# RWKV attention and a squared-ReLU layer on one core: steps 3 to 5 transposed by DMA, and new orders from step 3 on

## The chip, the core and the metric

The kernel runs on one core of a Trainium2 chip. The metric is the device time of one execution in microseconds (us). Several runs are taken and their median is the time; one further execution is recorded by the hardware profiler, and its span (first to last instruction) is a little shorter than its own time. The engines are TensorE (PE; PEld is its weight load), VectorE (DVE), ScalarE (ACT), GpSimd (POOL) and SyncE (SP), which here only issues DMAs.

## What is computed

Linear attention with a decaying state, then a layer with a squared ReLU. Batch 4, 8 heads, 768 tokens, 48 numbers a head; the layer goes from 384 to 2048 and back.

```python
def _attn_ref(r, k, v, w, u):
    state = zeros((B, H, D, D))
    for t in range(S):
        cur = einsum('bhd,bhe->bhde', u[None] * kt, vt)
        y[:, :, t] = einsum('bhd,bhde->bhe', rt, state + cur)
        state = wt[:, :, :, None] * state + einsum('bhd,bhe->bhde', kt, vt)

def _moe_ref(x, w_in, w_out):          # x: y as (4 * 768) x (8 * 48)
    h = x @ w_in
    r = maximum(h, 0.0)
    return (r * r) @ w_out
```

## The kernel before

**Steps.** The 3072 tokens go through in twelve steps s = 0 to 11 of 256 tokens, three to a batch. On the 128 partitions lie pairs of neighbouring tokens (j = 0, 1); the partitions are two chunks c of 64. Attention of later steps runs beside the layer of earlier ones.

**An order written out by hand.** The string ORDER (line 17) holds some 900 words, each one operation: a name, step and part, and then `:bank` (the PSUM bank) or `=A`, `=V`, `=G` (ScalarE, VectorE, GpSimd). The loop at line 634 records them in this order under a manual schedule. Each engine runs its own words strictly in the order of the string, and waits where an operand or a buffer isn't ready. SyncE's list too: a DMA whose source isn't ready holds up all DMAs behind it. Buffers are handed out in rotation by `buf` (line 173) in the order of the words: r, k, v and w have four each, rkT two, y_sb two, xT four.

**Attention of a step.** ld loads w, r, k, v (line 201). ww_ (288) multiplies the decays of a pair, lw_ (292) takes the logarithm, cum_ (332 to 336) sums it over the chunk on TensorE, from step 8 on with ni_ (344) on VectorE for one half; exp_ and ac_ (349, 356) take the exponential. rw_ and kw_ (300, 304) apply the decay inside a pair; rd_.s.0 and rd_.s.1 (370) make the decayed r and k. These must be transposed: in steps 0 to 3 by tr_ on TensorE through PSUM (379) and a copy rkt_ (384), from step 4 on by dtr_ (387), a DMA transpose from SBUF to SBUF. p_ (404) makes the scores, pm_ (412, 415) masks them, y_ multiplies by v (v_ at line 296 is its cast), yc_ adds the carried state, and yq_ the token's own term, for which ku_, qp_, q_ and vq_ (307, 312, 315, 318) prepare vq (all three of y at line 450). su_, ts_ and sn_ (426, 436, 440) carry the state on. ysb_ (486, 488) copies y out of PSUM. Then y is transposed: in steps 0 to 5 by yt_ on TensorE (496) and a copy xt_ (500), from step 6 on by dyt_ (503), a DMA transpose.

**The layer of a step.** m1_.s.g (513) makes two of 16 column blocks of h in one PSUM bank; rl_ (520, 522) takes the ReLU, sq_ (528, 530) the square of four blocks. In steps 0 to 4, m2_ (536) multiplies by w_out, os_ (542, 544) scales and store (614) writes out. From step 5 on a form with seven block products takes the place of m2_: sw_ (568) makes sums of blocks of the activations, pw_ (590) the seven products, cx_ and ow_ (595, 597, 609) put them together. tw_.1 to tw_.4 (555) make the sums of the blocks of w_out, once. The weights are loaded and cast at the beginning (221).

**Small-tile products.** p_, su_, y_, yq_ and yc_ use parts of the 128x128 array; m1_, m2_, pw_, tr_, yt_ and cum_ the whole.

Of the kernel before, what the change touches and what calls it, by code (L numbers as in the profile page):

```python
# [39 lines left out]
dtr_.5.0 m1_.3.1:3 qp_.5 ts_.4.1=V m2_.2.1.3 rl_.3.1=A rl_.3.7=V dtr_.5.1 p_.4.1:0 p_.4.0:1 os_.2.1=V m1_.3.3:1  # L40
pm_.4.0 vq_.4 store.1.1 m2_.2.0.2 ld.6.r rl_.3.3=A pm_.4.1 m1_.3.2:2 ld.6.k sn_.4.1 m1_.3.0:3 ld.7.r rl_.3.2=A ww_.6=G
ld.7.k sq_.3.1=A su_.5:1 y_.4:0 ts_.5.0=V ww_.7=G yc_.4 q_.5 yq_.4 store.1.0 p_.5.0:1 ysb_.4=A m1_.3.5:2 ld.6.v
rl_.3.0=V lw_.7 m2_.2.0.3 pm_.5.0 yt_.4:1 os_.2.0=A m1_.3.4:3 ld.8.w xt_.4=V lw_.6 ku_.6 rl_.3.5=V p_.5.1:1 rl_.3.4=A
cum_.7:0 pm_.5.1 ld.8.r m1_.3.6:0 exp_.7 vq_.5 m1_.4.3:1 sq_.3.0=A rw_.7=V ld.7.v cum_.6:1 m1_.4.1:3 rl_.4.3=A kw_.7=G
m1_.4.0:2 rl_.4.1=A store.2.1 m1_.4.5:1 rl_.3.6=A rl_.4.0=V sn_.5.0 exp_.6 m2_.3.1.0:3 rd_.7.0 kw_.6=G sq_.3.2=A
m2_.3.0.0:0 rd_.7.1 m2_.3.0.1 rw_.6=G rl_.4.5=A m2_.3.1.1 sq_.3.3=A ww_.8=G rd_.6.0 m2_.3.0.2 ac_.7 m1_.4.4:1 qp_.6
rd_.6.1 dtr_.6.0 m2_.3.0.3 ac_.6 m1_.4.2:2 v_.6=A dtr_.6.1 ku_.7 q_.6 v_.7=A su_.6:1 y_.5:0 ld.11.w os_.3.0=V yc_.5
ld.9.w rl_.4.4=V vq_.6 yq_.5 ld.8.k m2_.3.1.2 rl_.4.2=V ysb_.5=A m2_.3.1.3 rw_.8=V ts_.6.0=A store.3.0 yt_.5:1 sn_.6.0
ld.8.v os_.3.1=A m1_.4.7:0 xt_.5=A qp_.7 m1_.4.6:3 ts_.6.1=V sq_.4.2=A m1_.5.7:2 rl_.4.6=A p_.6.1:1 rl_.5.7=V
store.0.1 p_.6.0:0 rl_.4.7=A sn_.6.1 m1_.5.0:1 pm_.6.1 lw_.8 m1_.5.1:3 sq_.4.0=A ld.9.k ww_.9=G pm_.6.0 m1_.5.5:0  # L50
rl_.5.1=A m1_.5.4:2 dtr_.7.0 sq_.4.3=A rl_.5.0=V y_.6:1 sq_.4.1=V rl_.5.5=A su_.7:0 yc_.6 rl_.5.4=A kw_.8=V yq_.6 q_.7
m2_.4.0.0:3 ysb_.6=A m1_.5.6:2 v_.8=A ts_.7.0=V dyt_.6 vq_.7 cum_.8:1 rl_.5.6=A m2_.4.1.0:0 ni_.8=V sq_.5.0=A dtr_.7.1
m2_.4.0.1 tw_.1=V sn_.7.0 m2_.4.0.2 ac_.8 exp_.8 store.3.1 m2_.4.0.3 ww_.11=V ld.9.r lw_.9 m1_.5.3:1 ku_.8 os_.4.0=A
ld.10.w rd_.8.1 m2_.4.1.1 sq_.5.2=A ld.9.v m2_.4.1.2 ts_.7.1=V rl_.5.3=A tw_.3=V m1_.5.2:3 dtr_.8.1 qp_.8 m1_.6.3:2
rl_.5.2=A m1_.6.4:1 sq_.5.1=A rd_.8.0 m2_.4.1.3 rl_.6.3=A rl_.6.4=V p_.7.0:1 os_.4.1=A sw_.5.0.1=V p_.7.1:0 ku_.9
sq_.5.3=A dtr_.8.0 m1_.6.0:3 pm_.7.1 m1_.6.2:1 rl_.6.0=A m1_.6.7:0 pm_.7.0 sn_.7.1 m1_.6.1:2 rl_.6.7=A sw_.5.1.1=V
pw_.5.1:3 rl_.6.1=A sw_.5.1.2=V tw_.2=V rl_.6.2=A y_.7:1 su_.8:0 sq_.6.1=A yq_.7 yc_.7 sw_.5.0.2=V pw_.5.2:1 cx_.5.1=A
sw_.5.0.3=V ysb_.7=A sw_.5.1.3=V m1_.6.6:2 sw_.5.1.4=V sq_.6.0=A dyt_.7 sw_.5.0.4=V m1_.6.5:0 ow_.5.1=V tw_.4=V
rl_.6.6=A pw_.5.6 sw_.6.0.1=G store.4.1 rl_.6.5=A cum_.9:1 ld.10.k cx_.5.2=A pw_.5.5 ni_.9=V ld.11.k pw_.5.7 ts_.8.0=V
exp_.9 store.2.0 q_.8 rw_.9=G m1_.7.2:2 cx_.5.3=A ld.10.v ac_.9 m1_.7.5:0 kw_.9=V rl_.7.2=A vq_.8 rd_.9.0 pw_.5.3  # L60
rl_.7.5=A m1_.7.6:2 sq_.6.3=A rd_.9.1 dtr_.9.0 sn_.8.0 m1_.7.1:0 ow_.5.4=V ow_.5.2=V qp_.9 p_.8.0:1 dtr_.9.1 rl_.7.1=A
p_.8.1:0 m1_.7.0:1 sq_.6.2=A pm_.8.1 m1_.7.7:0 rl_.7.6=A ku_.10 pm_.8.0 pw_.5.4 v_.9=A pw_.6.1:2 rl_.7.7=A q_.9
ow_.5.3=A su_.9:1 rl_.7.0=A y_.8:0 sw_.6.1.1=V cx_.6.1=A yc_.8 sw_.6.0.2=V lw_.11 sw_.6.1.2=V yq_.8 ww_.10=V pw_.6.2:1
ysb_.8=A kw_.10=V m1_.7.3:0 ts_.9.0=A sw_.6.1.4=V dyt_.8 sq_.7.3=A ow_.6.1=V m1_.7.4:3 sn_.9.0 rl_.7.3=V pw_.6.6
sw_.6.0.3=G store.5.0 rl_.7.4=A ts_.9.1=V sq_.7.2=A ld.10.r p_.9.1:0 cx_.6.2=V p_.9.0:1 sw_.6.1.3=V ld.11.r vq_.9
pw_.6.5 pm_.9.0 lw_.10 store.4.0 m1_.8.4:0 sq_.7.1=A store.5.1 m1_.8.2:3 sw_.6.0.4=V ld.11.v rl_.8.4=A kw_.11=V
cum_.10:1 cx_.6.3=A pw_.6.7 rw_.10=G rl_.8.2=A ni_.10=V m1_.8.5:0 pm_.9.1 exp_.10 qp_.10 m1_.8.0:3 ac_.10 rd_.10.0
pw_.6.3 rl_.8.0=A cum_.11:0 sq_.7.0=A ow_.6.2=V rw_.11=G m1_.8.3:3 dtr_.10.0 rd_.10.1 m1_.8.1:1 rl_.8.5=A sn_.9.1
ow_.6.4=V ac_.11 dtr_.10.1 y_.9:1 rl_.8.3=A ni_.11=V sw_.7.0.1=G yq_.9 q_.10 yc_.9 pw_.6.4 ysb_.9=A sw_.7.1.1=V
pw_.7.1:3 exp_.11 sw_.7.0.2=V dyt_.9 sw_.7.1.2=G ow_.6.3=V m1_.8.6:0 sq_.8.1=A cx_.7.1=V rd_.11.0 m1_.8.7:2 store.6.0  # L70
ku_.11 rl_.8.6=A pw_.7.6 rd_.11.1 rl_.8.7=A pw_.7.2:0 v_.11=A rl_.8.1=V dtr_.11.1 qp_.11 p_.10.0:0 ow_.7.1=V v_.10=A
p_.10.1:1 pm_.10.0 m1_.9.0:2 cx_.7.2=A store.6.1 sq_.8.0=A m1_.9.1:1 dtr_.11.0 rl_.9.0=V vq_.10 pw_.7.5 sq_.8.2=A
pm_.10.1 m1_.9.2:2 su_.10:0 sw_.7.1.4=V rl_.9.2=A y_.10:1 sw_.7.0.4=V rl_.9.1=A sw_.7.0.3=V m1_.9.3:2 sw_.7.1.3=V
sq_.8.3=A ts_.10.0=V m1_.9.7:1 cx_.7.3=A sn_.10.0 pw_.7.7 sw_.8.1.1=V rl_.9.7=A rl_.9.3=A yq_.10 sw_.8.0.1=V yc_.10
ow_.7.4=V m1_.9.4:1 sw_.8.0.3=G sq_.9.0=V ysb_.10=A pw_.7.3 rl_.9.4=A dyt_.10 sw_.8.1.2=G pw_.7.4 sq_.9.1=A m1_.9.5:1
ow_.7.3=V ts_.10.1=V pw_.8.1:2 rl_.9.5=A ow_.7.2=V sn_.10.1 q_.11 p_.11.1:0 cx_.8.1=A p_.11.0:1 m1_.9.6:0 sw_.8.0.2=V
vq_.11 pm_.11.1 m1_.10.2:1 m1_.10.7:3 rl_.10.2=A rl_.9.6=V sw_.8.1.3=G pw_.8.6 pm_.11.0 sq_.9.3=A m1_.10.4:0 sq_.9.2=A
pw_.8.2:1 cx_.8.2=V sw_.9.0.1=V su_.11:0 ow_.8.1=V rl_.10.7=A y_.11:1 ts_.11.0=V pw_.8.5 rl_.10.4=V sn_.11.0
m1_.10.0:3 sw_.9.1.1=V yc_.11 sw_.8.1.4=V rl_.10.0=A sw_.9.0.2=V yq_.11 m1_.10.3:0 cx_.8.3=V ysb_.11=A sw_.9.1.2=V
sw_.8.0.4=V m1_.10.1:3 rl_.10.3=A dyt_.11 pw_.8.7 sq_.10.1=A rl_.10.1=V pw_.8.3 store.7.0 ow_.8.4=V sq_.10.0=A  # L80
m1_.10.6:3 store.7.1 m1_.10.5:0 sw_.10.0.1=V rl_.10.6=A ow_.8.2=V pw_.8.4 sw_.10.0.2=G rl_.10.5=V m1_.11.7:3 ow_.8.3=A
sw_.9.0.3=G sq_.10.3=A store.8.1 m1_.11.3:0 rl_.11.7=V m1_.11.1:1 sq_.10.2=A rl_.11.3=V m1_.11.2:3 sw_.9.1.3=V
rl_.11.1=A sw_.10.1.1=G m1_.11.0:0 rl_.11.2=A pw_.9.1:2 sq_.11.1=A sw_.10.1.2=G m1_.11.6:3 cx_.9.1=V rl_.11.0=V
pw_.9.2:1 sw_.10.0.3=G rl_.11.6=A sw_.10.1.3=V m1_.11.5:0 m1_.11.4:3 rl_.11.5=A sq_.11.3=V pw_.9.6 rl_.11.4=V
pw_.10.1:0 sq_.11.2=V cx_.9.2=A pw_.10.2:3 ow_.9.1=V sw_.9.0.4=V pw_.9.5 sw_.9.1.4=V sw_.10.0.4=V pw_.9.7 cx_.9.3=A
sw_.11.1.1=V sq_.11.0=A cx_.10.1=V pw_.9.3 sw_.11.1.3=G ow_.9.4=V ow_.10.1=V pw_.10.6 sw_.11.0.1=V pw_.10.5 ow_.9.2=V
sw_.11.0.2=G cx_.10.2=V store.9.0 pw_.9.4 cx_.10.3=V store.8.0 sw_.11.1.2=V pw_.11.2:1 sw_.10.1.4=G ow_.9.3=A
store.9.1 pw_.11.1:2 sw_.11.0.4=V pw_.10.7 sw_.11.1.4=G cx_.11.1=V ow_.11.1=V pw_.10.3 pw_.11.5 sw_.11.0.3=G
ow_.10.2=V store.10.0 pw_.11.6 cx_.11.3=V ow_.10.4=V pw_.11.3 cx_.11.2=A pw_.11.7 ow_.11.2=V store.11.0 pw_.10.4
# [586 lines left out]
```

## Time and profile before

| what | value |
|---|---|
| median of 3 runs | 180.04 us (179.58 to 180.71) |
| the profiled execution: time, span | 178.85 us, 177.0 us |
| its mean granted clock of TensorE | 0.998 |
| DMA traffic | 35.63 MB, mean 201 GB/s |
| HBM read, written | 25.17 MB, 4.72 MB |
| DMA transposes of r and k, of y | 16, 6 |
| transposes on TensorE of r and k (blocks), of y (blocks) | 64, 36 |

An engine's busy time counts its instructions' durations, not the time in which its sequencer waits or issues. A row of the chain of waits names the line that held the end at that time. TensorE's matmuls overlap, so a matmul's own duration is longer than the time it adds; the chain gives what a group of them adds. The lines that matter are shown in the prediction, where they are used.

### The profile page before, as it was taken

Reading aid. Unit: us, or ns where it says so; the run is one execution under the profiler, and the core shown is the slowest. Engines: PE = TensorE matmul, PEld = TensorE weight load, DVE = VectorE, ACT = ScalarE, POOL = GpSimd, SP = SyncE. Lnnn points to the kernel's source line nnn. Section 1 sums busy time; section 2 is a strip of 40 time slices with the busy share of each in tenths; the row PEclk is TensorE's granted clock in tenths of the full one; section 3 lists DMA queues with packets and bytes.
Section 4 is the critical chain, followed back from the end, with each engine's and each line's share of the span. In section 5 each row is a group of like instructions: output and inputs, shape, how many; then the busy total and the mean of one; then the engine's idle time right before and its main releaser. Section 6 shows DMA issues by size and latency. Waiting matters only on the chain.

```text
span 177.0 us, 5877 instructions
## 1 busy us (share of the span) xinstructions
PE 169.8 (96%) x2458; PEld 135.5 (77%) x2458; DVE 144.5 (82%) x228; ACT 136.9 (77%) x225; POOL 129.6 (73%) x117
## 2 busy tenths in 40 slices
...
GB/s 156 325 357 390 354 231 368 355 351 249 299 254 204 47 219 323 275 194 211 311 137 209 280 63 242 211 95 278 198 152 163 45 3 4 133 48 0 87 95 133
DMA packets 78811, 35.63 MB, mean 201 GB/s; under 512 B 72129, under 2 KB 77250, under 8 KB 78786
## 3 DMA queue, kind: packets, MB, share of 16 engines
...
HBM read 25.17 MB, written 4.72 MB: 169 GB/s over the span
## 4 chain that ended last, share of the span: by engine, by line
PE 73%; DVE 9%; DMA 7%; SPq 6%; issue 2%; POOL 1%; ACT 1%; ACTq 0%; DVEq 0%; POOLq 0%
PE one L513 29%; PE one L590 15%; PE one L536 15%; PE att L450 6%; DMA w_st_b<-in_moe_w_in_dram 5%; SPq L201 3%; DVE pmT_b L415 3%; PE att L404 3%; DMA r_b<-in_r_dram 2%; PE att L426 2%; DVE w_st_b L568 2%; SPq L209 1%; PE one L379 1%; DVE rdec_buf L370 1%; DVE q_b L315 1%
## 5 line engine op out<-in xcount | busy, mean ns | idle before, releaser
L513 PE MATMUL one<-xT_b,wi_sb 128*128 128x256 bf16 x576 | 70.8, 273 | 0.7 <-ACT gt_b L520 0.3
L513 PEld LDWEIGHTS <-wi_sb 128*128 128x128 f16 x576 | 54.9, 98 | 9.6 <-issue 1.5
L520 ACT ACTIVATE gt_b<-one 128x512 f16<-128x512 f32 x65 | 37.8, 596 | 12.1 <-PE one L513 11.2
L528 ACT ACTIVATE gt_b<-gt_b 128x1024 bf16<-128x1024 f16 x44 | 45.8, 1054 | 0.6 <-DVE gt_b L522 0.2
L536 PE MATMUL one<-wo_sb,gt_b 128*128 128x384 f16 x160 | 28.7, 326 | 0.0
L415 DVE TENSOR_TENSOR pmT_b<-att,mask 128x1024 bf16<-128x1024 f32 x22 | 26.2, 1214 | 1.3 <-PE att L404 1.3
L522 DVE TENSOR_SCALAR gt_b<-one 128x512 f16<-128x512 f32 x31 | 20.9, 685 | 5.4 <-PE one L513 4.4
L307 POOL TENSOR_TENSOR ku_b<-k_b,u_bc 128x768 f32<-128x768 f32 x12 | 22.4, 1869 | 3.0 <-DMA k_b<-in_k_dram 2.3
L440 POOL TENSOR_TENSOR S_b<-t_b,ac_buf 128x384 bf16<-128x384 f32 x20 | 18.1, 906 | 8.9 <-DVE t_b L436 4.5
L590 PEld LDWEIGHTS <-gt_b 128*128 128x128 bf16 x280 | 23.4, 98 | 0.6 <-issue 0.2
L312 POOL TENSOR_TENSOR ku_b<-ku_b,r_b 128x768 f32<-128x768 f32 x12 | 22.4, 1863 | 0.6 <-DMA r_b<-in_r_dram 0.4
L536 PEld LDWEIGHTS <-gt_b 128*128 128x128 bf16 x160 | 15.2, 98 | 9.2 <-issue 0.2
L318 POOL TENSOR_TENSOR vq_b<-v_b,q_b 128x768 bf16<-128x768 f32 x12 | 18.5, 1539 | 4.1 <-PE att L450 3.0
L590 PE MATMUL one<-wo_sb,gt_b 128*128 128x192 f16 x168 | 17.0, 246 | 0.0
L315 DVE TENSOR_REDUCE q_b<-ku_b 128x16 f32<-128x768 f32 x12 | 11.3, 945 | 3.7 <-POOL ku_b L312 3.7
L370 DVE TENSOR_TENSOR rdec_buf<-r_b,att 128x768 bf16<-128x768 f32 x12 | 11.4, 948 | 2.3 <-ACT att L349 1.8
L595 ACT ACTIVATE w_st_b<-one 128x192 f32<-128x192 f32 x13 | 4.3, 330 | 10.9 <-PE one L590 10.9
L300 POOL TENSOR_TENSOR r_b<-r_b,w_b 128x384 f32<-128x384 f32 x8 | 8.0, 1001 | 5.1 <-DMA r_b<-in_r_dram 5.1
L370 DVE TENSOR_TENSOR rdec_buf<-k_b,att 128x768 bf16<-128x768 f32 x12 | 11.4, 946 | 0.1
L568 POOL TENSOR_TENSOR gt_b<-gt_b 128x512 bf16<-128x512 bf16 x7 | 8.1, 1154 | 4.5 <-DVE w_st_b L568 4.0
L590 PE MATMUL one<-w_st_b,gt_b 128*128 128x192 f16 x112 | 11.2, 246 | 0.0
L488 ACT CAST y_sb_b<-att 128x768 bf16<-128x768 f32 x10 | 8.0, 799 | 3.8 <-PE att L450 3.6
...
## 6 DMA issues: line engine op xcount, KB each, us to landing
w_b<-in_w_dram SPq DMA_DIRECT2D x12, 384.0 KB, 5.3
r_b<-in_r_dram SPq DMA_DIRECT2D x12, 384.0 KB, 4.9
k_b<-in_k_dram SPq DMA_DIRECT2D x12, 384.0 KB, 5.8
v_b<-in_v_dram SPq DMA_DIRECT2D x12, 384.0 KB, 5.6
...
rkT_b<-rdec_buf SPq DMA_TRANSPOSE x16, 3.5
```

The source lines that it names most:

```text
L307: nc.gpsimd.tensor_mul(buf("ku", s)[:], buf("k", s)[:, :, 1:3, :], u_bc[:, :, None, :].to_broadcast([C, H, 2, D]))
L312: nc.gpsimd.tensor_mul(ku[:], ku[:], buf("r", s)[:, :, 0:2, :])
L318: nc.gpsimd.tensor_mul(buf("vq", s)[:].rearrange("p j h d -> p h j d"), buf("v", s)[:], buf("q", s)[:, :, :, None].to_broadcast([C, H, 2, D]))
L370: nc.vector.tensor_mul(rdec[:, i, :, heads, 0:D], x.rearrange("p h j d -> p j h d"), decay[:, None, :, :].to_broadcast([C, 2, n, D]))
L415: nc.vector.tensor_mul(pmT, ps_p[:].rearrange("p e (a x) -> p (e a) x", a=2), mk.to_broadcast([C, 4, 2 * C]))
L440: nc.gpsimd.tensor_mul(buf("S", s + c, 1 - c)[:], buf("t", s, c)[:].rearrange("p (a e d) -> p a e d", a=HP, e=2), tiles["a_c", s][:, :, c, ...
L513: nc.tensor.matmul(ps1[:, j, :], wi_sb[:, n // 4, kk, n % 4 * 128:(n % 4 + 1) * 128], xT[:, :, kk, :], start=(kk == 0), stop=(kk == KT - 1))
L520: nc.scalar.activation(rl, m1, AF.Relu, scale=RS)
L522: nc.vector.tensor_scalar(out=rl, in0=m1, scalar1=RS, scalar2=0.0, op0=ALU.mult, op1=ALU.max)
L528: nc.scalar.activation(gt, rl, AF.Square)
L536: nc.tensor.matmul(m2, gt[:, n, c * C:(c + 1) * C], wo_sb[:, n, :], start=(n == 0), stop=(n == NT - 1))
L590: nc.tensor.matmul(where_to, gt[:, n, :], wo[:, n, :], start=(n == 0 and i in (1, 2, 5)), stop=(n == NT // 2 - 1), skip_group_check=True)
```

## The change

Only ORDER changes: words from the 181st on (where the m2_ of steps 0 and 1 run) are put in another order, and with them the PSUM banks and the engines of some 80 operations. No function changes.

- Step 3: tr_.3.0, tr_.3.1 and the copies rkt_.3.0 (VectorE) and rkt_.3.1 (ScalarE) go; dtr_.3.1 and dtr_.3.0 come.
- Steps 4 and 5: yt_ and the copies xt_.4 (VectorE) and xt_.5 (ScalarE) go; dyt_.4 and dyt_.5 come.
- tw_.1 and tw_.3, which stood among the work of steps 7 and 8, stand beside that of step 3. All four tw_ stay on VectorE.
- Of the 56 sw_, 16 instead of 17 are on GpSimd, in part others than before.
- One matmul on zeros, warm_.1.5, stands behind the last product.

The part around steps 3 to 5:

```diff
-m2_.1.1.1 sn_.2.0 sq_.1.3=A m2_.1.0.1 cast.o.2=A m2_.0.1.1 ld.4.k qp_.3 cum_.3:0 y_.2:1 sq_.0.2=A yc_.2 yq_.2 ld.4.r
-q_.3 m2_.1.1.2 cast.o.3=A m2_.1.0.2 rw_.3=V ld.5.w ww_.4=G m2_.0.0.2 ysb_.2=V ac_.3 exp_.3 m2_.0.0.3 kw_.3=G ld.4.v
-m2_.1.1.3 rd_.3.0 os_.0.0=A lw_.4 v_.3=G m2_.1.0.3 ld.5.r rd_.3.1 os_.1.1=A yt_.2:1 kw_.4=G cum_.4:1 os_.1.0=V xt_.2=A
-tr_.3.0:0 ac_.4 su_.3:0 exp_.4 tr_.3.1:2 ld.5.v ts_.3.0=V rw_.4=G m2_.0.1.2 rkt_.3.0=V rkt_.3.1=A m1_.2.0:1 sn_.3.0
-ld.6.w rd_.4.0 m2_.0.1.3 ww_.5=G ts_.3.1=V m1_.2.6:2 ld.5.k os_.0.1=A rd_.4.1 v_.4=G m1_.2.3:0 ld.7.w ku_.4 p_.3.1:1
-rl_.2.3=A p_.3.0:0 pm_.3.1 m1_.2.1:3 lw_.5 rl_.2.0=A store.0.0 m1_.2.2:0 rl_.2.1=A dtr_.4.1 pm_.3.0 vq_.3 m1_.2.5:1
...
+m2_.1.1.1 sn_.2.0 sq_.1.3=A m2_.1.0.1 sq_.0.2=V cast.o.2=A m2_.0.1.1 ld.4.k qp_.3 y_.2:1 yc_.2 yq_.2 m2_.1.1.2 kw_.3=G
+ld.4.r q_.3 cast.o.3=A cum_.3:0 m2_.0.1.2 ysb_.2=V ww_.4=G m2_.0.0.2 exp_.3 m2_.1.0.2 ac_.3 rw_.3=G lw_.4 rd_.3.1
+m2_.1.1.3 v_.3=G m2_.1.0.3 os_.1.1=V dtr_.3.1 cum_.4:1 rd_.3.0 kw_.4=G os_.1.0=A yt_.2:0 exp_.4 m2_.0.0.3 xt_.2=V
+ku_.4 dtr_.3.0 ac_.4 m2_.0.1.3 os_.0.0=A rw_.4=V su_.3:0 store.0.0 m1_.2.4:1 ts_.3.0=A ld.4.v rd_.4.1 m1_.2.7:0
+sn_.3.0 ld.5.w rl_.2.4=A ld.5.r m1_.2.2:2 os_.0.1=A rd_.4.0 vq_.3 rl_.2.7=A m1_.2.0:3 ld.5.k ts_.3.1=V m1_.2.1:0
+rl_.2.2=V qp_.4 m1_.2.6:1 rl_.2.0=V rl_.2.1=A ld.5.v p_.3.1:1 sq_.2.0=A p_.3.0:0 pm_.3.1 m1_.2.5:0 v_.4=G ld.6.w
+rl_.2.6=A m1_.2.3:2 sn_.3.1 rl_.2.5=A pm_.3.0 m2_.2.1.0:3 rl_.2.3=A ww_.5=G sq_.2.1=A su_.4:1 tw_.1=V y_.3:0 ld.6.r
+yc_.3 sq_.2.2=A yq_.3 m2_.2.0.0:0 rw_.5=V dtr_.4.0 lw_.5 m2_.2.1.1 tw_.3=V ysb_.3=A m2_.2.0.1 sq_.2.3=A yt_.3:2
+ts_.4.0=V cum_.5:0 kw_.5=V m2_.2.1.2 dtr_.4.1 xt_.3=V exp_.5 ww_.6=G m2_.2.1.3 rd_.5.0 sn_.4.0 m1_.3.2:1 os_.2.1=A
...
+dtr_.5.0 rl_.3.6=A ku_.5 su_.5:0 rl_.3.3=A m1_.3.4:3 ts_.5.0=V rl_.3.0=A store.1.0 m1_.3.5:1 rl_.3.4=A ld.7.w vq_.4
+p_.4.1:0 ld.6.k p_.4.0:1 pm_.4.1 m1_.3.1:3 ld.7.k sn_.5.0 m2_.2.0.3 rl_.3.1=A pm_.4.0 m1_.3.7:2 qp_.5 rl_.3.5=A
+sq_.3.0=A p_.5.1:0 y_.4:1 pm_.5.1 rl_.3.7=A yc_.4 ww_.7=G sq_.3.1=A yq_.4 m2_.3.0.0:2 ysb_.4=V ku_.6 sq_.3.2=A
+cum_.6:0 q_.5 dyt_.4 p_.5.0:1 m2_.3.1.0:1 exp_.6 kw_.6=V m2_.3.0.1 qp_.6 os_.2.0=A ac_.6 m2_.3.0.2 store.2.0 sq_.3.3=A
+rd_.6.1 ld.6.v m2_.3.1.1 ld.7.r rd_.6.0 lw_.7 m2_.3.1.2 kw_.7=G m2_.3.0.3 pm_.5.0 dtr_.6.0 vq_.5 m1_.4.1:0 q_.6
+cum_.7:0 m1_.4.0:3 ac_.7 exp_.7 y_.5:1 dtr_.6.1 rl_.4.0=V yq_.5 rl_.4.1=V yc_.5 m1_.4.7:3 os_.3.0=V ysb_.5=A rw_.7=G
+m2_.3.1.3 rl_.4.7=A dyt_.5 ku_.7 m1_.4.6:0 rd_.7.0 v_.6=A m1_.4.2:3 rl_.4.6=A store.2.1 m1_.4.4:2 sq_.4.3=A ld.7.v
+rl_.4.2=V qp_.7 ld.8.w m1_.4.5:0 rd_.7.1 rl_.4.4=A ld.8.k m1_.4.3:3 sq_.4.0=A rl_.4.5=V ld.8.r su_.6:0 vq_.6 p_.6.0:1
...
+sq_.4.1=A vq_.7 yc_.6 dtr_.7.0 yq_.6 m1_.5.4:3 ysb_.6=V lw_.8 rl_.5.5=A m1_.5.0:2 kw_.8=G ts_.7.0=V rl_.5.4=A dyt_.6
...
+ow_.10.2=V pw_.11.6 sw_.11.0.3=V store.10.0 pw_.11.5 cx_.11.2=A ow_.10.3=A pw_.11.7 cx_.11.3=A store.10.1 pw_.11.3
+ow_.11.4=V pw_.11.4 ow_.11.2=V store.11.0 warm_.1.5 ow_.11.3=A store.11.1
```

More of the change, by code (lines that the diff above doesn't have):

```diff
@@ L40 @@
[L40 to L89, printed above, removed]
@@ new lines @@
+rd_.5.1 m2_.2.0.2 rw_.6=G rl_.3.2=A m1_.3.6:3 lw_.6 ts_.4.1=V dtr_.5.1 v_.5=A q_.4 m1_.3.0:2 sn_.4.1 ac_.5 m1_.3.3:1
+dtr_.5.0 rl_.3.6=A ku_.5 su_.5:0 rl_.3.3=A m1_.3.4:3 ts_.5.0=V rl_.3.0=A store.1.0 m1_.3.5:1 rl_.3.4=A ld.7.w vq_.4
+p_.4.1:0 ld.6.k p_.4.0:1 pm_.4.1 m1_.3.1:3 ld.7.k sn_.5.0 m2_.2.0.3 rl_.3.1=A pm_.4.0 m1_.3.7:2 qp_.5 rl_.3.5=A
+sq_.3.0=A p_.5.1:0 y_.4:1 pm_.5.1 rl_.3.7=A yc_.4 ww_.7=G sq_.3.1=A yq_.4 m2_.3.0.0:2 ysb_.4=V ku_.6 sq_.3.2=A
+cum_.6:0 q_.5 dyt_.4 p_.5.0:1 m2_.3.1.0:1 exp_.6 kw_.6=V m2_.3.0.1 qp_.6 os_.2.0=A ac_.6 m2_.3.0.2 store.2.0 sq_.3.3=A
@@ new lines @@
+rd_.6.1 ld.6.v m2_.3.1.1 ld.7.r rd_.6.0 lw_.7 m2_.3.1.2 kw_.7=G m2_.3.0.3 pm_.5.0 dtr_.6.0 vq_.5 m1_.4.1:0 q_.6
+cum_.7:0 m1_.4.0:3 ac_.7 exp_.7 y_.5:1 dtr_.6.1 rl_.4.0=V yq_.5 rl_.4.1=V yc_.5 m1_.4.7:3 os_.3.0=V ysb_.5=A rw_.7=G
+m2_.3.1.3 rl_.4.7=A dyt_.5 ku_.7 m1_.4.6:0 rd_.7.0 v_.6=A m1_.4.2:3 rl_.4.6=A store.2.1 m1_.4.4:2 sq_.4.3=A ld.7.v
+rl_.4.2=V qp_.7 ld.8.w m1_.4.5:0 rd_.7.1 rl_.4.4=A ld.8.k m1_.4.3:3 sq_.4.0=A rl_.4.5=V ld.8.r su_.6:0 vq_.6 p_.6.0:1
+ts_.6.0=A m1_.5.7:2 pm_.6.0 rl_.4.3=A m1_.5.5:0 sn_.6.0 rl_.5.7=A ld.9.w q_.7 m1_.5.6:3 os_.3.1=A v_.7=G sq_.4.2=A
```

42 lines of the change are left out of this document (38 added, 4 removed).

## The prediction

> **What bounds the kernel now.** I read the page's engine line and its chain first, then a table by stage, then the chain in order of time, and last the queue that issues the DMAs.
>
> ```profile
> PE 169.8 (96%) x2458; PEld 135.5 (77%) x2458; DVE 144.5 (82%) x228; ACT 136.9 (77%) x225; POOL 129.6 (73%) x117
> ...
> PE 73%; DVE 9%; DMA 7%; SPq 6%; issue 2%; POOL 1%; ACT 1%; ACTq 0%; DVEq 0%; POOLq 0%
> ```
>
> TensorE is busy for 96% of the span and carries 73% of the chain. An average hides where the rest lies, so the second view cuts the span into stages, from about where the two orders part (38 us) to the last matmul; its columns are busy time and instructions of each engine, granted clock, share of the DMA engines, GB/s.
>
> ```profile
> core 0: us, PE busy (x) PEld busy (x) DVE busy (x) ACT busy (x) POOL busy (x), PEclk, DMA share, GB/s
> ...
> 38.00:57.00 19.00, 19.00 (x297) 13.97 (x296) 12.92 (x18) 15.68 (x27) 16.00 (x15) 1.00 1.10 266
> 57.00:62.00 5.00, 5.00 (x38) 3.24 (x36) 4.37 (x7) 3.91 (x5) 4.92 (x4) 1.00 0.24 44
> 62.00:80.00 18.00, 18.00 (x292) 13.86 (x293) 14.37 (x18) 13.57 (x24) 15.01 (x14) 1.00 0.99 251
> 80.00:100.00 20.00, 20.00 (x296) 15.05 (x289) 17.84 (x24) 18.04 (x30) 16.95 (x12) 1.00 1.05 231
> 100.00:120.00 20.00, 19.92 (x356) 17.53 (x354) 19.04 (x35) 17.79 (x32) 11.77 (x10) 1.00 0.91 163
> 120.00:140.00 20.00, 19.80 (x316) 17.18 (x314) 19.49 (x31) 18.28 (x33) 15.42 (x12) 1.00 0.77 169
> 140.00:174.00 34.00, 33.83 (x436) 31.40 (x433) 26.19 (x55) 17.94 (x29) 17.62 (x16) 1.00 0.19 59
> ```
>
> From 38 us on TensorE idles 0.08 + 0.20 + 0.17 = 0.45 us in all, at full clock. So every microsecond of matmul that goes is worth a microsecond at the end, as long as no wait takes its place, and there is almost no idle time left to win. Two engines stand close behind: VectorE at 95 to 97% from 100 to 140 us, and the DMA engines at about 1.0 until 100 us, with one hole of 5 us from 57 to 62 us at 0.24.
>
> **The change, part by part.** The removed transposes are read from the chain in order of time (start, duration, what):
>
> ```profile
> 45.90 0.45 PE one L379 x8
> ...
> 46.79 0.55 PE one L379 x8
> ...
> 53.25 0.45 PE att L426 x16
> ...
> 62.63 0.76 PE one L513 x6
> ...
> 68.58 0.34 PE one L496 x6
> 68.91 0.66 PE one L513 x6
> ...
> 82.37 0.33 PE one L496 x6
> ...
> 173.87 0.04 issue
> 173.91 0.33 ACT w_st_b L595
> ```
>
> Step 3's two transposes took 0.45 and 0.55 us, those of y of steps 4 and 5 0.34 and 0.33 us. The 0.55 holds 0.1 us that TensorE loses whenever it comes back from the small-tile products of p_, su_ and y_ to full tiles: the same m1_ group takes 0.76 us behind p_ and 0.66 us elsewhere. That 0.1 us is not removed, since m1_.2.4 now stands behind su_.3 and pays it. What goes is therefore 0.45 + 0.45 + 0.34 + 0.33 = 1.57 us. Counting the changes from full to small tiles and back, the new order has 30 of them where the old has 29, which gives back about 0.1 us. The added warm_.1.5 is one matmul behind the last pw_; it runs beside the last scaling on ScalarE (0.33 us) and nobody waits for it, so it costs nothing; were it ahead of that scaling in the chain, it would cost at most its own few tenths. The tail behind the last matmul (scaling, store) is the same.
>
> The copies out of PSUM go too, one pair to each of two engines, and some 80 operations change engine:
>
> ```profile
> L520 ACT ACTIVATE gt_b<-one 128x512 f16<-128x512 f32 x65 | 37.8, 596 | 12.1 <-PE one L513 11.2
> L528 ACT ACTIVATE gt_b<-gt_b 128x1024 bf16<-128x1024 f16 x44 | 45.8, 1054 | 0.6 <-DVE gt_b L522 0.2
> ...
> L522 DVE TENSOR_SCALAR gt_b<-one 128x512 f16<-128x512 f32 x31 | 20.9, 685 | 5.4 <-PE one L513 4.4 <-ACT y_sb_b L488 1.0
> ...
> L292 ACT ACTIVATE lw_buf<-ww_b 128x384 bf16<-128x384 f32 x12 | 6.3, 524 | 2.2 <-DVE ww_b L288 1.9 <-POOL ww_b L288 0.2
> ...
> L384 ACT COPY rkT_b<-one 128x1024 bf16<-128x1024 bf16 x4 | 4.0, 1014 | 0.8 <-PE one L379 0.7
> ...
> L488 DVE CAST y_sb_b<-att 128x768 bf16<-128x768 f32 x2 | 1.9, 954 | 1.1 <-PE att L450 1.1
> ...
> L544 DVE TENSOR_SCALAR w_st_b<-one 128x384 f32<-128x384 f32 x3 | 1.6, 548 | 0.0
> ```
>
> Counted by these means, VectorE loses five relus (-3.4 us), gains two squares and two y copies (+3.8 us) and gives five scalings and some small work away: about -2 us over the run, ScalarE about -1.5 us. Neither sets the end, so this is worth nothing by itself, but it is slack where VectorE was fullest: up to the last product of step 7 the new list asks 3 us less of VectorE against TensorE's work than the old one. The sums of weight blocks were on VectorE and stay there; tw_.1 and tw_.3 (about 2 us together) move from step 7's neighbourhood to step 4's, where VectorE is busy 12.92 of 19.00 us, so I cost them at nothing; if that cover went they would cost at most themselves. GpSimd has one sum of activation blocks fewer, but its work comes 3 to 4 us later against TensorE's from step 7 on; it idles 8.2 us from 100 to 120 us, which covers that.
>
> Now what is added: four DMA transposes on SyncE's queue. The two source views (min, median, max of the issue in ns; then of issue to landing in us) show what such transposes cost:
>
> ```profile
> L387 SPq DMA_TRANSPOSE rkT_b<-rdec_buf x16: 1233/1279/3139, 53.0 to 134.3; - x16
> ...
> DMA to landing us min/median/max: 3.1/3.5/6.7
> ```
>
> ```profile
> L503 SPq DMA_TRANSPOSE xT_b<-y_sb_b x6: 1211/1212/2598, 90.3 to 150.8; - x6
> ...
> DMA to landing us min/median/max: 2.5/2.6/4.0
> ```
>
> Step 3 first. The timeline and the page's DMA list give its places:
>
> ```profile
> 42.93 1.12 SPq L201 DMA_DIRECT2D v_b<-in_v_dram  x1
> ...
> 44.34 0.95 DVE L370 TENSOR_TENSOR rdec_buf<-k_b,att 128x768 bf16<-128x768 f32 x1
> ...
> 50.54 0.64 PE L404 MATMUL att<-rkT_b 64*64 64x128 bf16 x32
> ```
>
> ```profile
> v_b<-in_v_dram SPq DMA_DIRECT2D x12, 384.0 KB, 5.6
> ```
>
> The second decayed operand of step 3 is ready at 44.34 + 0.95 = 45.29 us; in the new order os_.1.1 (0.55 us) stands between the two, so about 45.84 us. Landing takes 3.5 us: 49.3 us; at the longest row, 52.5 us. p_.3 ran at 50.54 us; ahead of it the new order has three more m1_ groups (3 x 0.66) and no transposes (-0.90), so it comes at 51.6 us. Cover: 2.3 us at the median, 0.9 us late at the longest. I take none, since only these two transposes are then under way.
>
> The wait is also SyncE's. Behind dtr_.3.1 and dtr_.3.0 are queued store.0.0, ld.4.v, ld.5.w, ld.5.r, ld.5.k, ld.5.v, ld.6.w and ld.6.r. The last issue ends at 45.84 + 1.28 = 47.1 us, so ld.4.v starts at least 4.2 us later than its 42.93 us. It lands near 47.1 + 5.6 = 52.7 us, its cast takes about 0.8 us, and su_.4, which needs it, moves from 53.25 us to 54.3 us: 0.8 us to spare.
>
> y of step 4: between its last product and m1_.4.1 TensorE has seven m2_ groups, cum_.6 and half of p_.5, about 5.3 us; the copy on VectorE takes 0.95 and the landing 2.6 (longest 4.0), 3.6 to 5.0 us. Step 5 has a like cover of 5.3 us. Both cost nothing; without cover each would cost its landing less the 0.34 us removed.
>
> A wait that I do expect: after y_.3 ScalarE has a rest of sq_.2.2 (up to 1.05), lw_.5 (0.52) and ysb_.3 (0.80, in the old trace as well), up to 2.4 us, while TensorE has three m2_ groups, 1.95 us, before yt_.3: 0 to 0.4 us. There are like places in step 5, where ScalarE's list runs without a gap (lw_.8 stands ahead of rl_.5.5, and a bank waits for that) and where several PSUM banks are asked for again within 0.1 to 0.3 us. I put 0.5 us on all of them; bounds: 0, and 1.5 us, the whole gain.
>
> Sum against the profiled execution: 177.0 us of span and 1.85 us around it, 178.85 us; -1.57 + 0.1 + 0.5 = -0.97, so **177.9 us**. The runs shown have a median of 180.04 us, 1.2 us above the profiled one, so I forecast **179.0 us** for the median.
>
> A page's rule speaks against this change. The Trainium skill (VectorE: DVE Perf Modes, The three transpose paths) puts a 128x128 block at 390 ns on TensorE and 1309 ns by DMA, and advises TensorE where PSUM will do. By that figure the eight blocks of one operand would take an estimated 10.5 us one after another. The rows above disagree: eight blocks land in 3.5 us, and TensorE streams eight in 0.45 us.
>
> **The rivals.** *All waits covered.* If nothing new is late and the 0.45 us of idle time goes with VectorE's lighter list, the gain is 1.57 + 0.45 - 0.1 = 1.9 us, 178.1 us. For it: the old order was as tight and idled only 0.45 us. Against: the places just named.
>
> *Waits eat the gain.* If the waits reach their bound of 1.5 us, or p_.3 is 0.9 us late and the rest 0.5, the time is 180.0 us.
>
> *Slower: the DMA queue falls behind.* SyncE issues in order, and the wait for step 3 moves every later load by 4.2 us; the four transposes add about 2 x 1.28 + 2 x 1.21 = 5.0 us of issue. The hole from 57 to 62 us gives back 0.76 x 5 = 3.8 us. What is left, some 4 us or more, shifts the loads of steps 6 to 9, and loads already come on demand:
>
> ```profile
> POOL r_b L300 <- DMA r_b<-in_r_dram: 5.1, 4, 2.7
> ```
>
> GpSimd idles 3.0 us from 62 to 80 us, and about as much from 80 to 100 us; as long as loads are less than 3 us late, that absorbs it. Beyond that point its products (q, then y) come late and TensorE waits, with 4.2 us as the price if none of it is absorbed: 180.04 - 1.5 + 4.2 = 182.7 us; with half of it 180.6 us. For it: the share of about 1.0 until 100 us. Against: the new order issues ld.11.w and ld.8.r later, which frees places in the queue.
>
> **How the numbers follow.** The forecast has 0.42, all waits covered 0.16, waits that eat the gain 0.12, the slower queue 0.30. A difference of 1% (1.8 us) is about what a measurement of this kernel tells from no change. Faster by more than that needs nearly all of the first rival: 0.15. Slower by more needs at least 3.3 us of the queue's price: 0.24, the greater part of that rival. Within 1%: 0.61. The likeliest case alone spans 178.5 to 179.6 us; the range that leaves out no more than 2 in 10 goes from 178.0 us, the first rival, to 182.5 us, just short of the queue's full price.
>
> **What would show it.** In the profile after: 1.57 us less of L379 and L496 on TensorE; idle time of TensorE after 38 us of about 0.5 to 1 us; p_.3 near 51.6 us with its transposes landed by 50 us; yt_.3 waiting for ysb_.3; VectorE under 95% from 100 to 140 us. The forecast is wrong if TensorE idles by more than 1.5 us, and wrong in its mechanism if the idle time stands behind q_, vq_ or v_ that waited for loads.

## The result, and the profile after

| what | before | after |
|---|---|---|
| median of 14 runs each | 179.71 us (179.30 to 180.71) | 178.50 us (177.55 to 179.60) |
| the profiled execution: time, span | 178.85 us, 177.0 us | 177.58 us, 175.8 us |
| its mean granted clock of TensorE | 0.998 | 1.000 |

The ratio is 0.993, with a 95% interval from 0.990 to 0.995: 0.7% faster, which lies within the 1% that the prediction counts as no change. The forecast, 179.0 against a median of 180.04 us, was a ratio of 0.994.

First the page of the new kernel, its engine line and its chain by engine:

```profile
PE 169.0 (96%) x2431; PEld 133.7 (76%) x2431; DVE 141.8 (81%) x221; ACT 135.4 (77%) x229; POOL 125.5 (71%) x116
...
PE 85%; SPq 5%; DMA 5%; issue 1%; ACT 1%; ACTq 0%
```

VectorE held 9% of the old chain and holds none of the new one; TensorE has 85% instead of 73%. The table by stage of the new kernel shows why (columns as in the prediction; the last stage ends at 173 us here):

```profile
38.00:57.00 19.00, 19.00 (x280) 13.36 (x279) 15.21 (x18) 14.83 (x25) 15.78 (x13) 1.00 0.89 229
57.00:62.00 5.00, 5.00 (x45) 3.61 (x44) 3.84 (x7) 4.13 (x7) 1.90 (x3) 1.00 1.15 241
62.00:80.00 18.00, 18.00 (x287) 12.87 (x285) 14.65 (x17) 13.35 (x26) 16.00 (x13) 1.00 0.98 211
80.00:100.00 20.00, 20.00 (x325) 15.36 (x322) 17.30 (x23) 18.16 (x29) 17.82 (x15) 1.00 1.04 241
100.00:120.00 20.00, 20.00 (x313) 17.49 (x310) 17.41 (x32) 18.32 (x31) 12.61 (x10) 1.00 0.86 193
120.00:140.00 20.00, 20.00 (x337) 17.60 (x335) 18.54 (x32) 16.30 (x32) 15.67 (x13) 1.00 0.97 196
```

TensorE is busy without a gap from 38 to 140 us; the 0.08 + 0.20 us that it idled from 100 to 140 us are gone, and VectorE is there at 17.41 and 18.54 of 20 us instead of 19.04 and 19.49. From 57 to 62 us the DMA engines, with a hole of 0.24 before, are at 1.15, since the loads now come then.

The chain in order of time gives the account. Before, from a point both orders share (the 24 m2_ products behind p_.2) to the last matmul:

```profile
35.45 4.01 PE one L536 x24
...
161.17 12.67 PE one L590 x152
173.84 0.03 ACTq L595
```

And after, with the places of step 3's p_ and of yt_.3 between:

```profile
35.56 4.01 PE one L536 x24
...
51.79 0.57 PE att L404 x32
...
57.91 0.34 PE one L496 x6
...
158.45 13.88 PE one L590 x168
172.33 0.03 ACTq L595
```

From that point to the last matmul it was 173.84 - 35.45 = 138.39 us, of which 0.28 us idle, and is 172.33 - 35.56 = 136.77 us, none of it idle. So matmul time fell by 138.11 - 136.77 = 1.34 us, and 0.28 us of waits went. Against that, the common point comes 0.11 us later (nothing ahead of it was changed; over all fourteen profiles of this document it lies anywhere from 35.26 to 37.55 us), and the tail behind the last matmul is 3.47 us instead of 3.16 us. The sum is -1.34 - 0.28 + 0.11 + 0.31 = -1.20 us, the difference of the spans.

Last, the source view of the second transpose of step 3 in the new kernel (in the window from 46 to 47.4 us):

```profile
L387 SPq DMA_TRANSPOSE rkT_b<-rdec_buf x1: 1237/1237/1237, 46.1 to 46.1; - x1
...
DMA to landing us min/median/max: 3.1/3.1/3.1
```

It landed at 49.2 us, 2.6 us before the p_ of step 3 at 51.79 us.

### The profile page after: what moved, and what is told of

The parts are those of the page before. It is cut to its first block, busy times and chain, and to the rows that moved or that the text cites. A ratio compares the mean times of both kernels' runs of the same rounds, so it can differ in the third digit from the quotient of the medians.

```text
span 175.8 us, 5827 instructions
## 1 busy us (share of the span) xinstructions
PE 169.0 (96%) x2431; PEld 133.7 (76%) x2431; DVE 141.8 (81%) x221; ACT 135.4 (77%) x229; POOL 125.5 (71%) x116
## 4 chain that ended last, share of the span: by engine, by line
PE 85%; SPq 5%; DMA 5%; issue 1%; ACT 1%; ACTq 0%
PE one L513 35%; PE one L590 19%; PE one L536 15%; PE att L450 7%; DMA w_st_b<-in_moe_w_in_dram 5%; SPq L201 4%; PE att L404 3%; PE att L426 2%; SPq L209 1%; PE att L334 1%; PE one L496 1%; PE att L336 1%; PE one L379 1%; PE att L332 0%; ACT gt_b L520 0%
## 5 line engine op out<-in xcount | busy, mean ns | idle before, releaser
L520 ACT ACTIVATE gt_b<-one 128x512 f16<-128x512 f32 x70 | 40.9, 596 | 10.2 <-PE one L513 9.3
L528 ACT ACTIVATE gt_b<-gt_b 128x1024 bf16<-128x1024 f16 x42 | 43.5, 1056 | 1.4 <-DVE gt_b L522 1.0
L440 POOL TENSOR_TENSOR S_b<-t_b,ac_buf 128x384 bf16<-128x384 f32 x20 | 16.8, 841 | 6.1 <-ACT t_b L434 5.4
L522 DVE TENSOR_SCALAR gt_b<-one 128x512 f16<-128x512 f32 x26 | 17.6, 687 | 2.8 <-PE one L513 1.8
L590 PE MATMUL one<-wo_sb,gt_b 128*128 128x192 f16 x168 | 16.2, 246 | 0.0
L370 DVE TENSOR_TENSOR rdec_buf<-r_b,att 128x768 bf16<-128x768 f32 x12 | 11.4, 949 | 2.4 <-POOL r_b L300 1.2
L370 DVE TENSOR_TENSOR rdec_buf<-k_b,att 128x768 bf16<-128x768 f32 x12 | 11.4, 949 | 1.9 <-ACT ac_buf L356 1.5
L300 POOL TENSOR_TENSOR r_b<-r_b,w_b 128x384 f32<-128x384 f32 x8 | 8.0, 1002 | 5.2 <-DMA r_b<-in_r_dram 5.2
L436 DVE TENSOR_TENSOR t_b<-S_b,att 128x384 f32<-128x384 bf16 x16 | 8.8, 549 | 3.0 <-POOL S_b L440 2.5
L288 POOL TENSOR_TENSOR ww_b<-w_b 128x384 f32<-128x384 f32 x7 | 8.1, 1159 | 4.0 <-DMA w_b<-in_w_dram 4.0
```

Of the source, the lines that this page charges most:

```text
L370: nc.vector.tensor_mul(rdec[:, i, :, heads, 0:D], x.rearrange("p h j d -> p j h d"), decay[:, None, :, :].to_broadcast([C, 2, n, D]))
L440: nc.gpsimd.tensor_mul(buf("S", s + c, 1 - c)[:], buf("t", s, c)[:].rearrange("p (a e d) -> p a e d", a=HP, e=2), tiles["a_c", s][:, :, c, ...
L520: nc.scalar.activation(rl, m1, AF.Relu, scale=RS)
L522: nc.vector.tensor_scalar(out=rl, in0=m1, scalar1=RS, scalar2=0.0, op0=ALU.mult, op1=ALU.max)
L528: nc.scalar.activation(gt, rl, AF.Square)
L590: nc.tensor.matmul(where_to, gt[:, n, :], wo[:, n, :], start=(n == 0 and i in (1, 2, 5)), stop=(n == NT // 2 - 1), skip_group_check=True)
```

## The experiments

Each is one edit of the new order or of the old one. Words are given as in ORDER; a word that stays marks the place. The kernel before was timed beside each group; its median was 179.36, 179.48 and 179.56 us in the three groups. The ratios are against it.

| edit | median us | ratio, 95% interval | span of its profile |
|---|---|---|---|
| new order, step 3 back on TensorE | 179.77 | 1.002 (0.999 to 1.005) | 177.6 |
| new order, y of 4 and 5 back on TensorE | 178.66 | 0.997 (0.995 to 0.999) | 176.5 |
| old order, y of 4 and 5 by DMA | 192.34 | 1.070 (1.066 to 1.074) | 190.1 |
| old order, step 3 by DMA | 181.66 | 1.012 (1.007 to 1.016) | 180.5 |
| new order, step 3's transposes issued twice | 184.68 | 1.030 (1.027 to 1.032) | 184.3 |
| new order, tw_.1 and tw_.3 late | 178.69 | 0.996 (0.993 to 0.999) | 176.7 |
| new order, without warm_.1.5 | 178.05 | 0.993 (0.990 to 0.996) | 176.8 |
| new order, unchanged | 177.62 | 0.990 (0.987 to 0.992) | 175.5 |
| old order, y of 4 and 5 by DMA, waits filled | 188.39 | 1.049 (1.046 to 1.052) | 185.8 |
| new order, ld.4.v ahead | 177.93 | 0.991 (0.988 to 0.994) | 176.2 |
| new order, three loads ahead | 179.07 | 0.996 (0.993 to 0.999) | 176.4 |
| new order, y of 3 by DMA too | 184.20 (180.79 to 186.62) | none | 184.8 |

The unchanged new kernel was run again in the second group: 0.990 there and 0.993 in the first measurement. A difference of 0.3% between groups is thus no difference. TensorE is without a gap from 38 to 140 us in that profile too, and from the common point to the last matmul it takes 136.8 us, as in the first.

### Step 3's transposes back on TensorE, in the new order

```diff
-dtr_.3.1
-dtr_.3.0
-m2_.0.1.3
+m2_.0.1.3 tr_.3.1:2
-su_.3:0
+su_.3:0 tr_.3.0:0
-ts_.3.0=A
+ts_.3.0=A rkt_.3.1=A
-rd_.4.1
+rkt_.3.0=V rd_.4.1
```

> The new order with step 3's r and k transposed on TensorE again (two groups of eight, two copies, no DMA transposes for step 3). If the end is set by TensorE's work alone, the 0.9 us comes back: about 0.5% slower than the new order, ratio to the old kernel near 0.998. If the waits of SyncE's queue for these two transposes cost something in the new order, less comes back, and the ratio stays near 0.993.

The time is outside what was expected (1.002, not 0.998). The span is 1.8 us longer than that of the new kernel. The two groups put back take 0.45 and 0.57 us in this run's chain. The rest are two waits of TensorE, 0.1 us behind the first row shown here and 0.6 us ahead of the last:

```profile
48.83 0.70 DVE rkT_b L384
...
66.50 5.93 DMA k_b<-in_k_dram
...
72.50 2.18 POOL ku_b L307
...
74.76 1.81 POOL ku_b L312
76.56 0.96 POOL k_b L304
77.52 1.44 POOL vq_b L318
78.97 0.04 issue
79.01 0.82 PE att L450 x20
```

The first wait is for a copy out of PSUM. The second is the rival of the prediction: a load of k lands at 72.43 us, GpSimd's list hangs on it, and yq_.5 waits 0.6 us for vq_.5. In the new kernel the same two rows stand on the timeline, of GpSimd and of TensorE:

```profile
75.18 1.47 POOL L318 TENSOR_TENSOR vq_b<-v_b,q_b 128x768 bf16<-128x768 f32 x1
...
77.04 0.36 PE L450 MATMUL att<-vq_b,ident 64*64 64x384 bf16 x4
```

There vq_.5 ends at 76.65 us, 0.39 us before TensorE takes it up. That is all that lay between the new order and the slower rival in this execution. In the profile of the run without warm_.1.5, whose order is the same up to there, it was not enough: GpSimd waited 0.7 us for a load of k, and TensorE 0.2 us for vq_.5.

### y of steps 4 and 5 back on TensorE, in the new order

```diff
-dyt_.4
-dyt_.5
-m2_.3.0.1
+m2_.3.0.1 yt_.4:3
-rd_.6.1
+rd_.6.1 xt_.4=V
-m1_.4.6:0
+m1_.4.6:0 yt_.5:2
-rd_.7.0
+rd_.7.0 xt_.5=V
```

> The new order with y of steps 4 and 5 transposed on TensorE again. TensorE alone: 0.67 us comes back, ratio to the old kernel near 0.997. If the two DMA transposes hold up loads or m1_, the ratio stays near 0.993 or falls.

The span is 0.7 us longer than the new kernel's 175.8 us, for the 0.34 + 0.33 us of the two groups, and TensorE is as busy as there from 38 to 140 us. From the common point to the last matmul the difference is 0.8 us. On a bound engine without gaps the removed instruction was worth its own time, to within 0.2 us.

### The DMA transposes alone, in the old order

Two kernels: y of steps 4 and 5 by DMA in the places of yt_, and step 3's r and k by DMA behind each rd_.

```diff
-yt_.4:1
+dyt_.4
-xt_.4=V
-yt_.5:1
+dyt_.5
-xt_.5=A
```

> The old order with one part of the change alone: y of steps 4 and 5 transposed by DMA at the places of the old transposes. If only TensorE's work counts, 0.67 us faster, ratio 0.996. If the place in the order is what covers the landing (2.6 us against 1.3 us between yt_.5 and the first m1_ of step 5), TensorE waits 1 to 3 us and the ratio is 1.003 to 1.015.

```diff
-tr_.3.0:0
-tr_.3.1:2
-rkt_.3.0=V
-rkt_.3.1=A
-rd_.3.0
+rd_.3.0 dtr_.3.0
-rd_.3.1
+rd_.3.1 dtr_.3.1
```

> The old order with step 3's r and k transposed by DMA, issued right behind the loads that stand there. If only TensorE's work counts, 0.9 us faster, ratio 0.995. If the loads ahead of them in the queue delay the landing (loads there land about 5 us after their issue), p_.3 comes 0.5 to 2 us late and y_.3 with it: ratio 0.998 to 1.006.

Both are slower than before, by 7.0% and by 1.2%, which is more than either expectation allowed. The old order has too little work between the source and the product that takes the result, and the landing takes longer there, with loads beside it: 4.2 and 4.7 us for step 3's two transposes, 3.1 us in the new order. With step 3 by DMA, the table of TensorE's waits in that run has

```profile
PE att L404 <- DMA rkT_b<-rdec_buf: 2.1, 1, 2.1
```

a wait of 2.1 us at p_.3. With y by DMA, m1_.4.3 and m1_.5.7 wait 3.8 and 3.6 us, since the transposes took 4.6 and 4.05 us and TensorE had 0.9 and 0.5 us of work left when they were issued. A third wait of 1.3 us follows near 111 us, where p_ waits for rd_ on VectorE. But 8.6 us of waits do not make the 13.0 us between the medians. The table by stage of this run shows the rest in the column of the granted clock, the third from the end:

```profile
70.00:75.00 5.00, 1.23 (x12) 0.81 (x10) 2.36 (x2) 2.06 (x3) 4.70 (x6) 0.88 1.19 249
75.00:80.00 5.00, 5.00 (x27) 3.40 (x26) 0.37 (x1) 2.25 (x4) 4.80 (x5) 0.50 0.78 227
...
90.00:94.00 4.00, 0.43 (x5) 0.14 (x4) 0.35 (x1) 2.89 (x5) 3.27 (x3) 1.00 1.16 290
94.00:98.00 4.00, 4.00 (x49) 2.82 (x50) 2.76 (x3) 0.00 (x0) 0.00 (x0) 0.57 1.17 232
```

Behind each of the two long waits the granted clock is at one half, for 5.8 and for 3.4 us of work, and the chain of the same run shows what that costs:

```profile
74.84 1.44 PE one L513 x6
...
77.03 3.78 PE one L513 x18
```

One m1_ group takes 1.44 us and three take 3.78 us, where the prediction's row has 0.66 us for one.

### The same with the waits filled by matmuls on zeros

```diff
-m1_.4.3:1
+warm_.16.1 m1_.4.3:1
-m1_.5.7:2
+warm_.15.2 m1_.5.7:2
```

> The old order with dyt_.4 and dyt_.5 in the places of yt_.4 and yt_.5, as in the run that took 192.34 us, but with 17 matmuls on zeros ahead of m1_.4.3 and 16 ahead of m1_.5.7, some 0.21 us each at full clock: TensorE is busy during the two waits of 3.8 and 3.6 us instead of idle, and nothing comes sooner. Theory: the granted clock of about 0.5 behind each wait is the price of the idle time. Then the clock stays near 1.00 there and the loss of 2.5 + 1.7 us of matmul time behind the waits goes: about 188 us, 1.045 of before. Rival: the clock falls for another reason (the DMA traffic at those times, or the time of the run): 192 us, 1.07.

It took 188.39 us, as the theory said. The same stages of this run (its second wait came earlier and is filled only in part), and the same groups in its chain:

```profile
70.00:75.00 5.00, 4.50 (x26) 2.39 (x25) 2.33 (x2) 1.83 (x3) 4.90 (x5) 1.00 1.14 251
75.00:80.00 5.00, 5.00 (x44) 3.77 (x42) 2.67 (x4) 3.93 (x7) 5.00 (x5) 1.00 0.76 217
...
90.00:94.00 4.00, 2.52 (x46) 1.61 (x45) 0.88 (x2) 0.02 (x1) 0.71 (x1) 1.00 1.11 241
```

```profile
74.74 0.81 PE one L513 x6
...
75.98 1.97 PE one L513 x18
```

m1_.4.3 starts at 74.74 instead of 74.84 us, so the transpose came no sooner. But the clock stays at 1.00, and the groups take 0.81 and 1.97 us. The traffic of the DMA engines at those times is much the same (1.14 and 1.11 for 1.19 and 1.16), so it is not what lowers the clock. The span fell by 4.3 us; 3.3 us of that are won by the end of the m1_ groups behind the second wait (96.38 for 99.67 us), the rest later, where the third wait of 1.3 us is gone, which the theory had not counted. A wait of TensorE of this length therefore has two prices: its idle time, and about half of it again or more in the slow matmuls behind it.

### Step 3's transposes issued twice, in the new order

```diff
-        nc.sync.dma_start_transpose(
-            out=buf("rkT", s)[:, i].rearrange("p j a t -> p (j a) t"),
-            in_=tiles["rdec", s][:, i].rearrange("t j h d -> t (j h d)"))
+        out = buf("rkT", s)[:, i].rearrange("p j a t -> p (j a) t")
+        for _ in range(2 if s == 3 else 1):
+            nc.sync.dma_start_transpose(out=out, in_=tiles["rdec", s][:, i].rearrange("t j h d -> t (j h d)"))
```

> The new order with each of step 3's two DMA transposes issued twice in a row: about 2.5 us more in SyncE's queue, so ld.4.v and the loads behind it start about 2.5 us later still. If the queue has the cover that the forecast gave it (p_.3 2.3 us, su_.4 0.8 us), p_.3 comes just in time and su_.4 about 1.7 us late, of which the later steps may win some back: 0 to 1.7 us slower than the new order, ratio to the old kernel 0.993 to 1.003. If the queue is already the bound, the whole 2.5 us appears: 1.007.

Much slower than either expectation. The tables of waits of this run, for TensorE and for SyncE's queue, say why (releaser, total us, times, longest):

```profile
PE att L404 <- DMA rkT_b<-rdec_buf: 4.9, 1, 4.9
```

```profile
SPq L389 <- DMA rkT_b<-rdec_buf: 4.0, 2, 2.3
```

The second transpose into the same buffer waits for the first to land, so the four took from 44.92 to 55.38 us on the queue. The run does not measure two more transposes, as was meant, but operands that land at 57.2 instead of 49.2 us. The cover of 2.6 us is used up, TensorE idles 4.9 us, and the clock is at 0.50 from 57 to 63 us. It shows how steep the fall behind the cover is, not what a transpose costs the queue.

### The weight sums late

```diff
-tw_.1=V
-tw_.3=V
-ni_.8=V
+ni_.8=V tw_.1=V
-ts_.7.1=V
+ts_.7.1=V tw_.3=V
```

> The new order with tw_.1 and tw_.3 back at the old places beside step 8's start. If VectorE is not a bound there any more, nothing changes: ratio near 0.993. If it is (about 2 us more in a stretch where it is 87 to 93% busy), TensorE waits up to 2 us: ratio up to 1.004.

In the same group the unchanged new kernel had 0.990, this one 0.996: about 1.1 us. The chain of this run shows TensorE's one wait from 80 to 100 us:

```profile
92.56 0.11 DVE w_st_b L555
92.66 1.35 DVE r_b L300
94.01 1.73 DVE rdec_buf L370 x2
95.74 0.48 DVE t_b L436
96.22 0.04 issue
96.26 0.64 PE att L404 x32
```

tw_.1 (L555) stands ahead of step 8's rw_ and rd_ on VectorE (L300, L370), everything behind it comes later, and p_.7 waits 0.8 us for ts_.7. So the new place of the two sums is worth 0.8 to 1.1 us in this order.

### Without warm_.1.5

```diff
-warm_.1.5 ow_.11.3=A
+ow_.11.3=A
```

> The new order without the matmul on zeros behind the last product. Nobody waits for it: no change, ratio near 0.993. If it does something for the tail, the last scaling or the end of the kernel moves by a few tenths of a us.

Its interval overlaps with that of the unchanged new kernel in the same group, and its ratio is the new kernel's first one: no effect that can be told.

### Loads ahead of step 3's transposes

One kernel moves ld.4.v behind ld.4.r, another ld.4.v, ld.5.w and ld.5.r.

```diff
-ld.4.r
+ld.4.r ld.4.v
...
-ld.4.v
```

> The new order with ld.4.v moved behind ld.4.r, ahead of step 3's two transposes, where SyncE's queue stands from 40.7 to 44.3 us. It lands before 47 us instead of at 52.9. Theory: the late loads cost nothing in the new order because TensorE never waits for one, so the time is that of the new order, 177.6 to 178.5 us (0.990 to 0.994 of before), with TensorE busy throughout. Rival: the hold of the queue is a cost: up to 0.5 us faster. Other side: the load shares the DMA engines with the transposes, these land more than 2.5 us later, p_.3 waits: slower by 1 us or more.

> The new order with ld.4.v, ld.5.w and ld.5.r ahead of step 3's transposes. Theory: what decides is how many loads are on the DMA engines when the transposes are issued. Three loads of 384 KB take some 4 us, so dtr_.3.1 is issued near 46 and lands near 49 to 50 us, dtr_.3.0 near 51, and p_.3 at 51.7 us is just met or waits for up to 1 us: 178 to 179.5 us (0.992 to 1.0). Rival: as in the old order with these transposes the loads push the landing past 52 us, TensorE idles 1 to 2 us and the half clock behind it adds as much: 180 to 181.5 us (1.003 to 1.01).

With one load ahead the time is the new kernel's, as far as the interval tells: that SyncE's queue stands until 44.3 us costs nothing that can be told. With three, the second transpose is issued at 47.14 us, takes 4.87 us and lands at 52.01 us. TensorE's waits in this run have the line

```profile
PE att L404 <- DMA rkT_b<-rdec_buf: 0.5, 1, 0.5
```

and the granted clock stays at 1.00 behind it. So the loads beside them set when transposes land, as the theory said. In this execution the wait of 0.5 us cost itself only (the span is 0.6 us longer); it is the shortest of eight, and why the median is 0.9 us above it isn't shown.

### y of step 3 by DMA too

```diff
-yt_.3:2
+dyt_.3
-xt_.3=V
```

> The new order with y of step 3 transposed by DMA too: yt_.3 and xt_.3 go (0.34 us of TensorE), dyt_.3 stands in their place on SyncE between the two transposes of step 4. y is copied by 57.6 us; 3 to 4.5 us to landing gives 61 to 62 us, and m1_.3 is reached at about 59.5 us. Theory: without cover the wait counts in full, and the lower clock behind it as well: 1.5 to 2.5 us idle, 1 us or more of clock, less 0.34: 180 to 182 us (1.0 to 1.013 of before). Rival: the queue slips it into the hole of the DMA traffic and it lands within 2.6 us: TensorE idles under 0.7 us and the time is that of the new order, about 178 us (0.99).

The four runs spread from 180.79 to 186.62 us. All are slower than each of the new kernel's twenty in the other groups (177.28 to 179.60 us), but only three are slower than every run of the old kernel in that group (178.81 to 181.14 us), so no ratio to it is given. The profiled run is the slowest, and it is 2.0 us late already at the common point (37.55 us), which is not the edit's doing. Its waits and its queue:

```profile
PE one L513 <- DMA xT_b<-y_sb_b: 4.4, 1, 4.4
```

```profile
58.89 3.92 SPq L387 DMA_TRANSPOSE rkT_b<-rdec_buf  x1
62.90 1.24 SPq L503 DMA_TRANSPOSE xT_b<-y_sb_b  x1
```

The transpose of y stood behind one of step 4's, which held the queue for 3.92 us (an issue takes 1.3 us at the median). The wait of 4.4 us was longer than expected for that reason, and the clock behind it was at 0.50 until 72 us, where 6.0 us of work lost an estimated 3.0 us. So 2.0 + 4.4 + 3.0 - 0.34 = 9.1 us, and the span is 9.0 us above the new kernel's. The other three runs have no trace.

## Why the prediction was right, point by point

**The bound.** Right. TensorE carries 85% of the new chain, and a matmul that goes is worth its own time: putting y of steps 4 and 5 back cost 0.7 to 0.8 us for 0.67 us of matmuls.

**The removed matmuls.** 1.57 us less 0.1 us for the changes of tile size were forecast, -1.47 us; the account above gives -1.34 us. The 0.13 us between was not traced to a group of matmuls.

**The transposes' cover.** Right, and to within 0.3 us. The forecast had the second rd_ of step 3 done at 45.84 us, the landing at 49.3, p_.3 at 51.6 us. Measured: issue at 46.1, landing at 49.2, p_.3 at 51.79 us. For steps 4 and 5 the waits list of the new kernel has no transpose either. The runs in the old order show that this cover decides: the same transposes without the new order lose 1.2% and 7.0%.

**New waits, +0.5 us.** This term was mis-sized: it measured nothing. The place named, yt_.3 behind ysb_.3, is not met: the copy ended at 57.55 us by ScalarE's timeline and yt_.3 comes at 57.91 us. With the old idle time going too, the mechanism was that of the first rival, "all waits covered". That rival's time, 178.1 us, was not reached: the matmuls gave 0.13 us less; the 0.45 us of old idle time were 0.28 us, as 0.16 us of the last stage's 0.17 us lay behind the last matmul, at 173.84 us; and 0.11 us at the common point and 0.31 us in the tail were lost where nothing was expected. The 0.11 us are within what that point varies by where nothing differs (35.26 us in the second profile of the same kernel). The 0.31 us are not chance: the tail is 3.2 to 3.3 us in the four profiles with the old order's end and 3.3 to 3.5 us in the ten with the new one's, with 3.4 us without warm_.1.5. The forecast had put that tail down as the same.

**The number.** That the forecast of -0.97 us lies so near to -1.20 us is in part luck. Of its three terms one, the new waits of 0.5 us, was not there; the losses just named, less the old waits that went (0.13 + 0.11 + 0.31 - 0.28 = 0.27 us), stood in for it, and the sum held none of them. Added to the median of 180.04 us, -0.97 us gives 179.1 us, where the prediction wrote 179.0.

**VectorE's sums at nothing.** Right for the new place, whose cover held. What was not priced is the old place: left there they cost 0.8 us of TensorE's time in the new order.

**The slower rival.** Its mechanism is real, but its point of decision was not one lateness of 3 us. In the new order ld.4.v came 5.1 us later (issued at 48.07 us by SyncE's timeline, at 42.93 us before), and of the steps that the rival spoke of ld.7.v 8.7 us later (at 81.08 us for 72.42 us), and TensorE did not wait for them. Yet vq_.5 had only 0.39 us to spare, and the run with step 3 on TensorE lost 0.6 us there. The late loads themselves are not due to the transposes alone: in that run ld.4.v is issued at 47.93 us, since store.0.0 stands ahead of it until 47.47 us. And the price was taken without the granted clock, which a wait of several microseconds lowers behind it.

**The rule that spoke against the change.** The Trainium skill (VectorE: DVE Perf Modes, The three transpose paths) gives 1309 ns for a 128x128 block by DMA; eight one after another, an estimated 10.5 us, would have put step 3's second operand at 56.6 us. It landed in 3.1 us; the measurement decides. The Trainium skill's advice for TensorE (the same page, Rules for kernel authors) held where less work stood between source and user than the landing took, 4.05 to 4.7 us in the two runs in the old order: there the DMA path lost.

No run beat the new kernel. The ones nearest to it, with ld.4.v ahead and without warm_.1.5, can't be told from it. Whether the tail's 0.31 us comes back with another end of the order wasn't tried.
